# A recurrence and a gated mixture on one core: the mixture's U half decoded and begun first, V of three blocks later from operands kept in DRAM

## The chip, the cores and the metric

One core of a Trainium2 chip runs the whole program. Its engines are TensorE (PE, matrix products, with its weight loads shown apart as PEld), VectorE (DVE), ScalarE (ACT) and GpSimd (POOL); SyncE (SP) issues most of the DMA transfers. The metric is the device time of one execution in microseconds (us), lower is better. The times given are those of several runs of the same kernel; one further execution was recorded by the profiler.

## The reference

Two stages, one feeding the other. The first is a linear recurrence over 768 tokens, for 4 batches and 8 heads of 40 channels, with a 40x40 state:

```python
for t in range(S):
    y[:, :, t] = einsum('bhd,bhde->bhe', r_t, state)
    Sa = einsum('bhde,bhe->bhd', state, a_t)
    state = state * w_t[:, :, None, :] - einsum('bhd,bhe->bhde', Sa, b_t)
    state = state + einsum('bhd,bhe->bhde', v_t, k_t)
x = y.transpose(0, 2, 1, 3).reshape(4, 768, 320)
```

The second is a gated mixture on x. The hidden layer's first 512 columns are U, the other 512 are V:

```python
h = maximum(x @ w_in, 0)                 # (4, 768, 1024)
u, v = h[..., :512], h[..., 512:]
v_n = (v - mean(v)) / sqrt(var(v) + 1e-6)
v_s = einsum('ts,bsd->btd', w_spatial, v_n) + b_spatial[None, :, None]
return (u * v_s) @ w_out                 # (4, 768, 320)
```

The product with w_spatial mixes all 768 tokens of a batch, so it can begin for a batch only when V of the rows that it reads is there, and its result is multiplied by U.

## The kernel before, in words

*Phase 1.* The tokens are cut into chunks of 64. A step (0 to 23) handles one chunk for two batches at once: 12 steps for batches 0 and 1, 12 for batches 2 and 3. Eight heads stand as 4 pairs, so a step has 8 units (2 batches x 4 head pairs), the two heads of a pair on the two halves of the partitions.

Three kinds of work belong to a chunk. Its *preparation*: loads (prep_piece), running products on VectorE (scan1, scan2), at_mul and sl_mul, then a product of 32x32 blocks on TensorE (lprime) whose result lblock copies from a PSUM bank to the tile Lc on VectorE, multiplied by the table maskl, which is -1 below the diagonal and 0 elsewhere. For four chunks together invert(g) then inverts these triangles on VectorE, in 30 pairs of a multiply and an add with one transpose ahead and two behind: its result XT is read by b_zt. Then the *block work* b_... of the chunk, on TensorE with copies on ScalarE and triangles cut out by GpSimd. Last the *chain* c_..., which alone hangs on the step before: c_bp (the state enters), c_ff, c_xx, c_mp (the state leaves as Mc) and c_y, each followed by its copy. y, the recurrence's output, is stored to the DRAM tensor xs by y_store, every second step, for 128 tokens. c_ff reads the tiles Rt and At; a part of Rt is the token load vtok_load, which goes from DRAM straight into it.

*The mixture's first layer.* A block is 128 tokens of one pair of batches: 12 blocks, and block j can be loaded after step 2j+1. m_load brings x from xs with six loads (tile xt), m_split cuts it into a high and a low part (xh on ScalarE, xl and the rest of xh on GpSimd), and then come four U products (m_u, a slot of 8 matmuls into a bank) and two V products (m_v, 8 wider matmuls). Both go to the tile pv or itmp. U is stored to the DRAM tensor uts; V is normalised (m_n1, m_root, m_n2, m_n3) and stored to vns. The weights w_in come as pairs of words and are decoded into wh and wl by six generators of eight pieces each, V's three first, one in a step from 4.2 on; only after all six does open_act open the pool in which the blocks' tiles stand. There are 72 slots for these products, at the times of M1 to M4 of each step from 11 on, four a step: 52 of them fall in steps 11 to 23, and 20 at times of 24 and later.

*What sets the order.* Phase 1's order is written out by hand: at(t, fn) puts calls into the list plan, which is sorted by t (the number ahead of the point is the step), and runs through it, issuing to each engine in that order. Each engine, and SyncE's queue, works its own instructions in the order in which they were issued. Entries with t of 24 and more are issued outside the hand-written part, and there a scheduler of the framework interleaves them with phase 2 by its own estimate.

*Phase 2.* For each of four batches and two halves of 384 tokens: spatial (72 products of vh, vl with the split w_spatial into the banks pg, then bias and U on VectorE, split again) and proj (36 products with w_out, tile po), whose result ot is stored once for a half. vload brings V of a batch by six row blocks (raw), splits them on ScalarE (vh) and GpSimd (vl), and loads U (ut).

The lines that the prediction names: L179 to L181 the three products of spatial, L199 the products of proj and L201 the output's store, L339 lprime, L349 lblock, L363, L367 and L372 the inversion, L384 the token load, L406 the triangles on GpSimd, L468 b_l21, L487 b_zt, L545 c_bp, L563 c_ff, L581 c_xx, L654 c_y's copy, L666 y_store, L685 and L689 m_load, L712 m_v, L759 m_u, L776 the copy xf, L51 and L55 the two splits, wherever they are called from.

## Time and profile before

| what | value |
| --- | --- |
| time, median of 3 runs | 667.46 us (665.67 to 667.48) |
| the profiled execution's own time | 665.08 us |
| its span | 663.3 us, mean granted clock 0.943 |
| busy: TensorE, VectorE, ScalarE, GpSimd | 571.8, 448.4, 384.2, 225.9 us |
| first product of step 0, 1, 7, 11, 12, 23 | 32.2, 65.5, 186.8, 255.1, 278.4, 476.6 us |
| y of step 23 written | 490.0 us |
| first product of proj, last product | 546.4, 659.2 us |

The span is the time from the first to the last recorded instruction; the time of a run is a little longer. A step's beginning is read from the first product of c_bp. Busy time of PE counts products whose ends are modelled. The granted clock is TensorE's, as a share of full speed. In a row of the groups, what stands behind the second bar is the idle time of the engine just before these instructions, and what ended it.

### The profile page before, as it was taken

To read this page: it belongs to the slowest core of one execution; us is meant where nothing else is said; L and a number is where in the kernel's file an instruction comes from. 1 tells how busy PE (TensorE), PEld (TensorE's weight loads), DVE (VectorE), ACT (ScalarE), POOL (GpSimd) and SP (SyncE) were. 2 spreads that over 40 slices of the span, in tenths; PEclk is the share of its full clock that TensorE was granted. 3 is DMA by queue.
4 is the path that set the end of the run, shared out by engine and by line. 5 is a ranking of instruction groups with operands and counts; after the bars stand their busy time and mean duration, and the time that the engine had idled before them with its cause. 6 is when DMAs were issued, how large, how long until landed. Compare 5 with 4: busy or idle time off the path is not lost.

```text
span 663.3 us, 25848 instructions
## 1 busy us (share of the span) xinstructions
PE 571.8 (86%) x10960; PEld 518.3 (78%) x10960; DVE 448.4 (68%) x970; ACT 384.2 (58%) x860; POOL 225.9 (34%) x298
## 2 busy tenths in 40 slices
PE   1447885498777887999999999999989999999997
PEld 1437674487766776888888888888878999999997
DVE  8999789989999999488896677343384842332220
ACT  2135662377666775688878887888765543221212
POOL 6013330224332334144341332332354843352221
PEclk9967997789787898999999999999998999999999
DMA  8654778477555546657565365375395557150001
GB/s 199 121 107 67 134 152 147 70 175 155 135 127 115 131 117 120 142 127 172 154 190 148 86 173 144 90 198 132 89 262 182 162 155 240 61 157 31 31 31 59
DMA packets 106331, 87.68 MB, mean 132 GB/s; under 512 B 35496, under 2 KB 92072, under 8 KB 104296
## 3 DMA queue, kind: packets, MB, share of 16 engines
q1 hardware_dynamic: 105672, 84.31, 52.0%
q10 hardware_dynamic: 544, 1.72, 1.2%
q8 instruction: 86, 1.41, 1.0%
q14 instruction: 29, 0.24, 0.1%
HBM read 59.20 MB, written 20.50 MB: 120 GB/s over the span
## 4 chain that ended last, share of the span: by engine, by line
PE 63%; DVE 15%; DMA 7%; issue 6%; ACT 4%; SPq 3%; POOL 1%; DVEq 0%; ACTq 0%; POOLq 0%
PE po L199 6%; PE pv L759 6%; PE pv L712 6%; PE pg L179 5%; PE pg L180 5%; PE pg L181 5%; PE ch L563 4%; PE bp L545 4%; PE ch L581 4%; PE bk L429 2%; DMA ein<-in_early 2%; DVE itmp L363 2%; PE bk L451 2%; PE bk L399 2%; PE bp L641 2%
## 5 line engine op out<-in xcount | busy, mean ns | idle before, releaser
L406 POOL TENSOR_SCALAR_AFFINE_SELECT Rt<-Rt 64x512 f32<-64x512 f32 (+1 forms) x144 | 83.8, 584 | 156.2 <-ACT Rt L592 128.5
L406 POOL TENSOR_SCALAR_AFFINE_SELECT At<-At 64x512 f32<-64x512 f32 x48 | 41.5, 864 | 164.0 <-ACT At L416 151.9
L555 ACT ACTIVATE Rt<-bp 64x416 f32<-64x416 f32 x96 | 49.1, 511 | 56.2 <-PE bp L545 53.6
L363 DVE TENSOR_TENSOR itmp<-A 128x30 f32<-128x30 f32 (+9 forms) x180 | 66.5, 369 | 3.4
L179 PE MATMUL pg<-wsh,vh 128*128 128x384 f32 x192 | 65.4, 341 | 2.0 <-ACT vh L51 2.0
L545 PE MATMUL bp<-lin,Mc 40*64 40x104 f32 x768 | 47.3, 278 | 22.1 <-DVE y L654 19.8
L183 DVE TENSOR_TENSOR g<-pg,bb 128x384 f32<-128x384 f32 x32 | 17.8, 556 | 70.7 <-PE pg L181 68.4
L180 PE MATMUL pg<-wsl,vh 128*128 128x384 f32 x192 | 65.1, 339 | 0.0
L181 PE MATMUL pg<-wsh,vl 128*128 128x384 f32 x192 | 63.6, 339 | 0.0
L367 DVE TENSOR_TENSOR A<-A,itmp 128x30 f32<-128x30 f32 (+9 forms) x180 | 59.1, 328 | 6.2
L545 PEld LDWEIGHTS bp<-lin,Mc 40*64 40x64 f32 x768 | 40.7, 150 | 25.5 <-DVE y L654 22.7
L563 PE MATMUL ch<-Rt,At 128*64 128x104 f32 x768 | 48.0, 283 | 5.9 <-issue 4.8
L55 POOL TENSOR_TENSOR gl<-g,gh 128x384 fp32r<-128x384 f32 x32 | 33.0, 1035 | 58.1 <-ACT gh L51 58.1
L592 ACT ACTIVATE Rt<-ch 64x416 f32<-64x416 f32 x96 | 49.1, 511 | 4.6 <-PE ch L581 2.2
L563 PEld LDWEIGHTS ch<-Rt,At 128*64 128x64 f32 x768 | 42.2, 157 | 10.4 <-issue 7.1
L51 ACT ACTIVATE gh<-g 128x384 fp32r<-128x384 f32 x32 | 16.7, 521 | 54.3 <-DVE g L184 54.3
L339 PE MATMUL bk<-at,sl 64*32 64x32 f32 x1536 | 21.2, 203 | 26.5 <-DVE sl L324 20.7
L55 POOL TENSOR_TENSOR vl<-raw,vh 128x512 fp32r<-128x512 f32 x24 | 31.5, 1324 | 31.6 <-ACT vh L51 30.1
L581 PE MATMUL ch<-ffs,xf 64*64 64x104 f32 x768 | 41.7, 261 | 0.0
L339 PEld LDWEIGHTS bk<-at,sl 64*32 64x32 f32 x1536 | 17.7, 114 | 29.5 <-issue 14.4
L179 PEld LDWEIGHTS pg<-wsh,vh 128*128 128x128 f32 x192 | 36.6, 190 | 2.4 <-ACT vh L51 2.2
L630 DVE TENSOR_TENSOR Mc<-ch,scn 104x160 f32<-104x160 f32 x44 | 18.5, 436 | 29.0 <-PE ch L619 18.7
(132 smaller groups left out, 1497.8 us busy)
## 6 DMA issues: line engine op xcount, KB each, us to landing
ein<-in_early SPq DMA_DIRECT2D x108, 129.0 KB
lin<-in_late SPq DMA_DIRECT2D x48, 160.0 KB
At<-at SPq DMA_DIRECT2D x48, 128.0 KB
uts<-ur SPq DMA_DIRECT2D x48, 128.0 KB
vns<-vr SPq DMA_DIRECT2D x24, 256.0 KB
raw<-vns SPq DMA_DIRECT2D x24, 256.0 KB
ut<-uts SPq DMA_DIRECT2D x24, 256.0 KB
Rt<-in_vtok SPq DMA_DIRECT2D x48, 80.0 KB
```

The lines of the kernel that those rows point to most:

```text
L55: eng.tensor_tensor(out=lo, in0=x, in1=hi.bitcast(F32), op=ALU.subtract)
L179: nc.tensor.matmul(pg, lhsT=vh[:, dc], rhs=w_h, start=(i == 0), stop=False)
L180: nc.tensor.matmul(pg, lhsT=vh[:, dc], rhs=w_l, start=False, stop=False)
L181: nc.tensor.matmul(pg, lhsT=vl[:, dc], rhs=w_h, start=False, stop=(i == NT - 1))
L363: nc.vector.tensor_tensor(out=tp, in0=A[:, k + 1:, k:k + 1].broadcast_to([P, m, k]), in1=A[:, k:k + 1, 0:k].broadcast_to([P, m, k]), op=AL ...
L367: nc.vector.tensor_tensor(out=A[:, k + 1:, 0:k], in0=A[:, k + 1:, 0:k], in1=tp, op=ALU.add)
L406: nc.gpsimd.affine_select(out=t, in_=t, pattern=[[0, k], [1, C]], base=0, channel_multiplier=-1, compare_op=ALU.is_gt, fill=0.0,)
L545: nc.tensor.matmul(bp[PR[par], q, :], lhsT=Mc[RR[par], n, :], rhs=li[RR[par], n, C:], start=(q == 0), stop=False, skip_group_check=True,)
L555: nc.scalar.activation(Rt[par][PR[par], gp, :], st["bp", g][PR[par]], AF.Copy)
L563: nc.tensor.matmul(ff[PR[1 - par], q, :], lhsT=At[par][:, n, :], rhs=Rt[par][:, n, :], start=True, stop=True,)
L581: nc.tensor.matmul(xx[ev, q, :], lhsT=xf[ev, n, :], rhs=ffs[ev, q, :], start=True, stop=True,)
L592: done = nc.scalar.activation(Rt[par][PR[par], gp], xx[PR[1 - par]], AF.Copy, scale=-1.0)
```

## The change

Six things are changed; all else that the diff shows follows from them.

1. *Decoding and pools.* U's three weight decodes come first (at 3.83, 4.43 and 5.69), V's three later (7.02, 8.2 and 9.6), from a pool of their own. The blocks' pool opens after the first three, a second one for V's tiles after the other three.
2. *U of blocks 0 to 2 first.* Twelve slots are new, from 7.8 to 10.9, and hold all U products of blocks 0 to 2. V of these blocks comes behind the U and V of blocks 5, 6 and 8 (the list ORDER). For that m_keep stores xh and xl of such a block to the DRAM tensor xsp (640 KB), and m_again loads them again. From step 11 on there are four slots a step as before, so that 64 fall ahead of step 24 and 8 behind; the last six are put at 24.8 or later.
3. *Triangles.* lblock is a copy on ScalarE with the factor -1, without the table. The upper triangle is zeroed instead inside invert: five memsets on A after the first transpose, on VectorE for the first group, on GpSimd for the others.
4. *Idle products.* beat issues 10 products of ident with itself (512 columns, result unused) at 0.415, ahead of b_zt of chunk 0.
5. *Times of the preparation.* The tables PREP, LPQ, GAP, INV_T and OV set when the later chunks are prepared and inverted; scr_store of the first chunks moves ahead.
6. *Output stores.* Each 128 rows of the output are stored by themselves, 24 stores for 8.

Branches that were never taken (for example the VectorE variant of c_xx_out) are taken out of the text, which changes no instruction.

```diff
-        nc.sync.dma_start(
-            out=out[b, h * TH:(h + 1) * TH].rearrange("(j p) n -> p j n", p=P), in_=ot
-        )
+            t0 = h * TH + j * P
+            nc.sync.dma_start(out=out[b, t0:t0 + P], in_=ot[:, j, :])
...
+    J_U = 3
+    xsp = dscr.tile([J_U, P, 5, NB, P], F32, name="xsp")
...
-        nc.vector.tensor_tensor(
-            out=Lc[:, u0:u0 + NU, :], in0=st.pop(("pl", s)),
-            in1=maskl.unsqueeze(1).broadcast_to([P, NU, HB]), op=ALU.mult,
-        )
+        nc.scalar.activation(Lc[:, u0:u0 + NU, :], st.pop(("pl", s)), AF.Copy, scale=-1.0)
...
-        A = inv.tile([P, HB, HB], F32, name="A")
+        Af = inv.tile([P, HB * HB + HB], F32, name="A")
+        A = Af[:, 0:HB * HB].rearrange("p (t s) -> p t s", s=HB)
         nc.vector.transpose(out=A, in_=Lc.rearrange("p u t -> p t u"))
+        h = HB // 2
+        while h:
+            x = Af.rearrange("p (b x) -> p b x", x=2 * h * (HB + 1))[:, :, h:h + h * HB]
+            (nc.gpsimd if g else nc.vector).memset(x.rearrange("p b (r c) -> p b r c", c=HB)[:, :, :, 0:h], 0.0)
+            h //= 2
...
+    def m_keep(j, *key):
+        xh, xl = st["xhl", key]
+        nc.sync.dma_start(out=xsp[j, :, 0:3], in_=xh.bitcast(F32))
+        nc.sync.dma_start(out=xsp[j, :, 3:5], in_=xl.bitcast(F32))
+
+    def m_again(j, *key):
+        xh = st["act"].tile([P, 3, NB, P], F32R, name="xh", bufs=2)
+        xl = st["act"].tile([P, 2, NB, P], F32R, name="xl", bufs=2)
+        nc.sync.dma_start(out=xh.bitcast(F32), in_=xsp[j, :, 0:3])
+        nc.sync.dma_start(out=xl.bitcast(F32), in_=xsp[j, :, 3:5])
+        st["xhl", key] = (xh, xl)
...
-        vr = st["act"].tile([P, DH], F32, name="vr", bufs=2)
+        vr = st["actv"].tile([P, DH], F32, name="vr", bufs=3)
...
+    def beat(k):
+        for _ in range(k):
+            nc.tensor.matmul(
+                st["beat"], lhsT=ident, rhs=ident.unsqueeze(1).broadcast_to([P, 4, P]), start=True, stop=True
+            )
...
+    for t, k in [[0.415, 10]]:
+        at(t, beat, k)
...
-    T_DEC, T_MOE = 4.2, 11
-    for i in range(6):
-        gen = decode(1 - i // 3, i % 3)
-        for k in range(8):
-            at(T_DEC + i + k * 0.10 - (0.9 if k == 0 else 0), step, gen)
-    at(T_DEC + 5.9, open_act)
-    slots = [T_MOE + k // 4 + (M1, M2, M3, M4)[k % 4] for k in range(3 * NS)]
+    T_DEC, T_DECV, T_MOE = (3.83, 4.43, 5.69), (7.02, 8.2, 9.6), 11
+    for half, t_dec, dk, lead in ((0, T_DEC, 0.08, 0.9), (1, T_DECV, 0.08, 0.45)):
...
+    slots = [7.8, 8.3, 8.55, 8.8, 9.3, 9.46, 9.8, 9.85, 10.3, 10.55, 10.7, 10.9]
+    slots += [T_MOE + k // 4 + (M1, M2, M3, M4)[k % 4] for k in range(3 * NS - len(slots))]
+    slots[-6:] = [max(t, NS + 0.8 + 0.05 * k) for k, t in enumerate(slots[-6:])]
...
-    for j in range(NS // 2):
+    ORDER = [("u", j) for j in range(J_U)]
+    for j in range(J_U, NS // 2):
+        ORDER += [("uv", j)] + [("v", k) for k, a in enumerate((5, 6, 8)) if a == j]
...
-        own = slots[6 * j:6 * j + 6]
-        at(max(own[0] - 1.6, 2 * j + 2.1, T_DEC + 5.92), m_load, bq, i)
-        at(max(own[0] - 0.45, 2 * j + 2.7), m_split, bq, i)
+        if kind == "v":
+            at(own[0] - 0.8, m_again, j, bq, i)
+        else:
+            at(max(own[0] - 0.9, 2 * j + 2.1, T_DEC[2] + 7 * 0.08 + 0.02, slots[4 * J_U - 4] - 0.4 if j == J_U else 0), m_load, bq, i)
+            at(max(own[0] - 0.5, 2 * j + 2.7), m_split, bq, i)
...
+        if kind == "u":
+            at(own[0] + 0.3, m_keep, j, bq, i)
...
```

How the order moves, at three places. The first is TensorE in step 9, between c_ff and c_xx of the chain (before: L563 is c_ff, L451 and L468 are block work of chunk 10, L581 is c_xx, L487 is b_zt of chunk 10). Before:

```order
L563 MATMUL ch<-Rt_134,At_3447 64x104
L563 MATMUL ch<-Rt_135,At_3448 64x104
L451 MATMUL bk<-ident,sl 128x128 x8
L468 MATMUL bk<-sl,at 32x32 x16
L581 MATMUL ch<-ffs,xf_131 64x104 x16
L487 MATMUL bk<-XT_3281,l_3919 32x32 x16
```

And now (L552 is c_ff, L440 and L457 are the block work, L570 is c_xx, L757 is a U slot):

```order
L552 MATMUL ch<-Rt_131,At_3499 64x104
L552 MATMUL ch<-Rt_132,At_3500 64x104
L440 MATMUL bk<-ident,sl 128x128 x8
L757 MATMUL pv<-xh,wh 128x256 x3
L757 MATMUL pv<-xl,wh 128x256 x2
L757 MATMUL pv<-xh,wl 128x256 x3
L457 MATMUL bk<-sl,at 32x32 x16
L570 MATMUL ch<-ffs,xf_128 64x104 x16
```

A U slot of eight products now stands among the block work, ahead of c_xx.

The second is SyncE's queue behind the y of step 23 (L666 stores y, L685 and L689 load a block, L154 loads a row block of V for phase 2, L762 stores U, L749 stores V, L164 loads U for phase 2). Before:

```order
L666 DMA xs<-y_8628 40x4x128 x2
L666 DMA xs<-y_8638 40x4x128 x2
L154 DMA raw<-vns 128x512 x2
L762 DMA uts<-ur 128x256
L164 DMA ut_9398<-uts 128x4x128
L749 DMA vns<-vr 128x512
L685 DMA xt<-xs 128x2x128
L749 DMA vns<-vr 128x512
L689 DMA xt<-xs 64x128
L762 DMA uts<-ur 128x256 x2
L689 DMA xt<-xs 64x128
```

And now (L645 stores y, L671 and L675 load a block, L760 stores U, L747 stores V):

```order
L645 DMA xs<-y_8901 40x4x128 x2
L645 DMA xs<-y_8911 40x4x128 x2
L671 DMA xt<-xs 128x2x128
L675 DMA xt<-xs 64x128 x2
L671 DMA xt<-xs 128x2x128
L675 DMA xt<-xs 64x128 x2
L760 DMA uts<-ur 128x256
L747 DMA vns<-vr 128x512 x2
L154 DMA raw<-vns 128x512 x2
```

The last block's six loads now stand straight behind the stores of y on which they wait, and the loads of V's row blocks behind them.

The third is TensorE after step 23, inside spatial of the first batch, ahead of the first product on row block 2 of V (vh02). Before, where xh_8815 is the third last block, block 9:

```order
L181 MATMUL pg1_9479<-wsh0_9268,vl00_9365 128x384
L179 MATMUL pg1_9479<-wsh1_9274,vh01_9370 128x384
L180 MATMUL pg1_9479<-wsl1_9275,vh01_9370 128x384
L181 MATMUL pg1_9479<-wsh1_9274,vl01_9371 128x384
L759 MATMUL pv_8858<-xh_8815,wh_138 128x256 x3
L759 MATMUL pv_8858<-xl_8816,wh_138 128x256 x2
L759 MATMUL pv_8858<-xh_8815,wl_139 128x256 x3
L179 MATMUL pg0_9407<-wsh2_9280,vh02_9376 128x384
```

And now, where xh_9119 is the last block, block 11:

```order
L181 MATMUL pg1_9533<-wsh1_9328,vl01_9425 128x384
L757 MATMUL pv_9124<-xh_9119,wh_135 128x256 x2
L757 MATMUL itmp_9136<-xh_9119,wh_135 128x256 x2
L757 MATMUL pv_9124<-xh_9119,wh_135 128x256
L757 MATMUL pv_9124<-xl_9120,wh_135 128x256 x2
L757 MATMUL pv_9124<-xh_9119,wl_136 128x256 x3
L757 MATMUL itmp_9136<-xh_9119,wh_135 128x256
L757 MATMUL itmp_9136<-xl_9120,wh_135 128x256 x2
L757 MATMUL itmp_9136<-xh_9119,wl_136 128x256 x3
L179 MATMUL pg0_9461<-wsh2_9334,vh02_9430 128x384
```

U products of the last block now stand ahead of the first product on vh02, where there stood one of block 9.

More of the change, by code (lines that the diff above doesn't have):

```diff
@@ L847, in phase1 @@
             at(t0 + (t1 - t0) * k / (INV_N - 1), step, gen)
-    T_DEC, T_MOE = 4.2, 11
-    for i in range(6):
-        gen = decode(1 - i // 3, i % 3)
-        for k in range(8):
-            at(T_DEC + i + k * 0.10 - (0.9 if k == 0 else 0), step, gen)
-    at(T_DEC + 5.9, open_act)
-    slots = [T_MOE + k // 4 + (M1, M2, M3, M4)[k % 4] for k in range(3 * NS)]
+    T_DEC, T_DECV, T_MOE = (3.83, 4.43, 5.69), (7.02, 8.2, 9.6), 11
+    for half, t_dec, dk, lead in ((0, T_DEC, 0.08, 0.9), (1, T_DECV, 0.08, 0.45)):
+        for i in range(3):
+            gen = decode(half, i)
+            for k in range(8):
+                at(t_dec[i] + k * dk - (lead if k == 0 else 0), step, gen)
@@ new lines, in phase1 @@
+    for j in range(J_U, NS // 2):
+        ORDER += [("uv", j)] + [("v", k) for k, a in enumerate((5, 6, 8)) if a == j]
+    n = 0
+    for kind, j in ORDER:
+        bq, i = j // 6, j % 6
+        own = slots[n:n + {"u": 4, "v": 2, "uv": 6}[kind]]
+        n += len(own)
+        if kind == "v":
[3 more added lines that the diff above has]
+            at(max(own[0] - 0.5, 2 * j + 2.7), m_split, bq, i)
+        us = {"u": own, "v": [], "uv": [own[k] for k in (0, 1, 3, 4) if k < len(own)]}[kind]
+        vs = {"u": [], "v": own, "uv": own[2::3]}[kind]
+        for t, d in zip(us, range(DH // P)):
@@ L883, in pads @@
         eng.memset(t[:, WF:], 0.0)
+    st["beat"] = ps_m.tile([P, DH], F32, name="pv")
     with tc.manual_schedule():
@@ L890, in phase1 @@
         pads(v, ein[1])
-        p.memset(maskl, -1.0)
-        for q in range(P // HB):
-            rows = slice(q * HB, (q + 1) * HB)
-            p.affine_select(
-                out=maskl[rows], in_=maskl[rows], pattern=[[1, HB]], base=0,
-                channel_multiplier=-1, compare_op=ALU.is_gt, fill=0.0,
-            )
         pads(p, ein[2])
@@ L937, in phase1 @@
         prep_load(4, 48)
-        for q in range(GS):
-            scr_store(q)
         b_lka(0)
```

131 lines of the change are left out of this document (54 added, 77 removed).

## The prediction

> **What bounds the kernel now.** I read first the busy times by stretch, cut at the first product of a step (step 0 begins at 32.2, step 1 at 65.5, step 11 at 255.1, step 23 at 476.6), then the waits, then the chain of waits, then the instructions in order of time around three places. The stretches (columns: stretch, length, busy time and count of TensorE products, weight loads, VectorE, ScalarE, GpSimd, granted clock, DMA share, GB/s):
>
> ```profile
> 32.20:65.50 33.30, 20.29 (x477) 18.36 (x474) 30.62 (x64) 15.61 (x37) 9.40 (x10) 0.64 0.50 88
> 65.50:186.80 121.30, 89.48 (x2664) 78.60 (x2656) 108.17 (x210) 71.75 (x164) 36.00 (x49) 0.89 0.70 137
> 186.80:255.10 68.30, 57.02 (x1600) 50.43 (x1600) 66.25 (x132) 48.75 (x111) 21.56 (x33) 0.90 0.50 120
> 278.40:476.60 198.20, 197.26 (x4350) 170.91 (x4344) 129.34 (x335) 161.58 (x365) 67.77 (x104) 1.00 0.53 142
> 489.30:541.80 52.50, 50.55 (x299) 48.34 (x298) 34.75 (x84) 27.78 (x60) 30.15 (x26) 0.97 0.59 176
> 541.80:663.30 121.50, 117.42 (x721) 117.03 (x719) 30.20 (x56) 29.31 (x61) 37.70 (x35) 1.00 0.29 94
> ```
>
> Up to step 10 VectorE sets the pace: 66.25 of 68.30 us busy in steps 7 to 10, while TensorE has 11.3 us idle there. From step 12 on TensorE is busy 197.26 of 198.20 us, and it stays the bound to the end: every product that leaves it after 278 is time. The waits of VectorE from 58 to 256 and of TensorE from 58 to 283, and the group that the first belong to:
>
> ```profile
> DVE Lc L349 <- PE bk L339: 4.0, 4, 1.8
> DVE Mc L630 <- ACT Rt L592: 2.3, 2, 1.4
> PE bk L468 <- DVE Lc L349: 5.2, 1, 5.2
> L349 DVE TENSOR_TENSOR Lc<-bk,maskl 128x256 f32<-128x256 f32 x24 | 10.1, 419 | 5.5 <-PE bk L339 5.5
> ```
>
> The copy Lc stands in VectorE's way twice: it costs 0.419 us, and VectorE waits in front of it for its product; once TensorE in turn waited 5.2 us for the bank that Lc empties.
>
> **The change, part by part.** The sum is made against the profiled execution's 665.1 us (span 663.3).
>
> *Triangles to ScalarE.* Fifteen of the 24 copies lie between 65 and 255 (1 in step 11, 4 before step 0, 4 after): 15 x 0.419 = 6.3 us leave VectorE, and with them up to 4.0 us of waits. On ScalarE a copy costs about 0.41 (next row), 0.4 us a step beside 12 to 13 busy of 18, so other work hides it; without that cover it would be the same 6 us. The zeroing runs on GpSimd (busy 21.56 of 68.30) and is needed only by the transpose at the inversion's end; group 0's, on VectorE, is 496 columns, at 485 ns for 512 about 0.6 us, and replaces four Lc of the prologue: even. I take -6.3: bounds -10.3 (the waits go too) and 0, since in steps 1 to 6 VectorE is idle for 13 of 121 us and so not always the one that is late.
>
> The copies xf of the same size on ScalarE, the one timed zeroing of 512 columns, and four more stretches (steps 8 to 11):
>
> ```profile
> L776 ACT ACTIVATE xf<-XT 128x256 f32<-128x256 f32 x24 | 9.9, 413 | 11.6 <-DVE XT L372 11.4
> L881 DVE MEMSET ein<- 128x512 f32 x1 | 0.5, 485 | 0.0
> 205.30:223.30 18.00, 16.00 (x432) 14.31 (x432) 17.51 (x36) 12.98 (x30) 5.53 (x8) 0.81 0.70 157
> 223.30:241.50 18.20, 14.63 (x402) 12.91 (x402) 17.65 (x36) 12.59 (x28) 4.83 (x8) 0.91 0.39 86
> 241.50:255.10 13.60, 12.79 (x400) 11.32 (x400) 13.05 (x29) 11.48 (x27) 5.46 (x9) 1.00 0.44 120
> 255.10:278.40 23.30, 18.48 (x362) 16.22 (x362) 14.21 (x26) 12.53 (x29) 6.90 (x10) 0.85 0.75 141
> ```
>
> *Twelve U products early.* One falls in step 7, three in step 8, four each in 9 and 10. A U takes 0.95 to 1.14 us, a V 1.85 to 2.04 (chain, below). TensorE's idle time: 2.0 us in step 8 (needs 2.9), 3.6 in step 9 (needs 3.8), 0.8 in step 10 (needs 3.8). Excess 4.1; the half-clock stretches of these steps (0.81, 0.91) will shrink as TensorE fills, so I take +3.5. Bounds 0 and +5.
>
> From the chain of waits (start, length, engine, tile and line; L712 are V's products, L759 are U's):
>
> ```profile
> 257.08 6.47 DMA Rt<-in_vtok
> 263.68 3.00 PE ch L563 x30
> 271.29 2.04 PE pv L712 x8
> 274.42 1.14 PE pv L759 x8
> 493.81 4.06 DMA raw<-vns
> 503.89 1.85 PE pv L712 x8
> 505.74 0.95 PE itmp L759 x8
> 518.14 0.17 PE pg L179
> ```
>
> *Step 11.* It lasts 23.3 us. The instructions in order of time show c_ff (L563) standing 4.5 us (3.42 and 1.12) for the second token load of step 11, issued only at 257.08, behind the six loads of the first block; step 10's had been issued at 234.77, 6.7 us ahead of that step:
>
> ```profile
> 261.99 0.58 PE L563 MATMUL ch<-Rt,At 128*64 128x104 f32 x2 [3.42 <-issue]
> 263.68 0.62 PE L563 MATMUL ch<-Rt,At 128*64 128x104 f32 x4 [1.12 <-DMA Rt<-in_vtok]
> 234.77 0.59 SPq L384 DMA_DIRECT2D Rt<-in_vtok  x1
> ```
>
> Now the first block loads come four steps earlier, and step 10 is 3 us longer, so the token load has more time. I take -4.0; bounds -5.7 (a step of 17.6) and +4.5 (the new stores and reloads, 640 KB a block, hold it up as much again).
>
> *Steps 12 to 23.* 52 slots before held 35 U and 17 V, now 31 and 21: 4 x 0.9 = +3.6.
>
> *After step 23.* 13 U and 6 V stood there, now 5 and 2: 8 x 0.95 + 4 x 1.85 = -15.0 us of TensorE's own work. But the cover of a chain goes with it. The last block's U wait for y of step 23, its store, the block load and the split. Rows:
>
> ```profile
> 489.24 0.75 DVE L654 TENSOR_TENSOR y<-bp,Et 104x256 f32<-104x256 f32 x2
> 491.48 2.23 SPq L666 DMA_DIRECT2D xs<-y  x4
> 476.23 0.39 SPq L685 DMA_DIRECT2D xt<-xs  x1
> 478.49 1.12 SPq L689 DMA_DIRECT2D xt<-xs  x2
> 481.22 0.85 ACT L51 ACTIVATE xh<-xt 128x768 fp32r<-128x768 f32 x1 [0.38 <-DMA xt<-xs]
> 483.55 0.87 POOL L55 TENSOR_TENSOR xh<-xt,xh 64x256 fp32r<-64x256 f32 x1
> 497.04 0.39 SPq L685 DMA_DIRECT2D xt<-xs  x1
> 511.32 0.83 ACT L51 ACTIVATE xh<-xt 128x768 fp32r<-128x768 f32 x1
> 498.57 0.44 PE L179 MATMUL pg<-wsh,vh 128*128 128x384 f32 x1 [1.95 <-ACT vh L51]
> ```
>
> On the old times: y ends at 490.0; four stores take 2.2 to issue (492.2) and about 2 to land (from the last xt issue's end at 479.61 to xh 1.6; a raw load in the chain 4.06): 494.2. A block's first load to its last operand (476.23 to 484.42) is 8.2: ready at 502.4. TensorE comes to the last block's first U after 24 gating products of 0.17 (chain, 518.14) and one U, at 489.4 + 4.1 + 0.95 = 494.5, and stands until 502.4: 7.9 us. Behind it in TensorE's order stand all further gating products; in ScalarE's, vh of row blocks 2 to 5 stands behind this xh; on SyncE their loads stand behind the block load. The old wait of 1.95 at this place is covered by it, so +5.9, and +1 for a longer time at half clock: +6.9. Bounds +2 (only xh must wait, 4.0 net of the old wait) and +14 (a load like the last one of before, 497.04 to 511.32).
>
> *Idle products.* Before step 0's first product on X, TensorE stands while VectorE inverts, and then runs at half clock:
>
> ```profile
> 52.45 1.06 PE L487 MATMUL bk<-XT,l 32*32 32x32 f32 x32 [12.27 <-DVE XT L372]
> 56.42 3.04 PE L581 MATMUL ch<-ffs,xf 64*64 64x104 f32 x32
> 75.24 1.64 PE L581 MATMUL ch<-ffs,xf 64*64 64x104 f32 x32
> ```
>
> Sixteen products of 104 columns take 1.6 at full and 3.0 at half clock, two running at once, so one of 512 columns by estimate 1.0 or 1.9, ten 10 or 19: against 12.3 idle they fit only if the clock rises under them. The gain is 1.4 + 0.5 at most, and VectorE is busy 30.62 of 33.30 there: I take -0.7, bounds -1.9 and +7. [...]
>
> *Output stores per 128 rows.* The end waits for the last store; a third of its size saves, by estimate, 0.5 of the 3.6 us from its issue at 659.7 to 663.3.
>
> ```profile
> 659.72 0.37 SPq L201 DMA_DIRECT2D out_y<-ot  x1
> ```
>
> *The rest.* The decodes are the same instructions in another order, the preparation of later chunks moves by up to a third of a step, and the mask tables leave GpSimd's prologue. I cost them at nothing: VectorE's other work hides the prologue's, and the counts stay; bounds -1 and +1, VectorE's idle time in steps 8 and 9 together (0.49 and 0.55).
>
> Sum: -6.3 + 3.5 - 4.0 + 3.6 - 15.0 + 6.9 - 0.7 - 0.5 = -12.5, so 652.6 in a run like the profiled one. That one lies 2.4 below the median of the runs shown (667.5) and 0.6 below the lowest; I take half of it: **653.5**.
>
> **Rivals.** (1) *The wait after step 23 eats the tail.* For it: SyncE issues the load straight behind the stores, and DMA is 59% busy there. Against it: a load at 476 took 5.0 to xh in the same crowd. With +14 for +6.9: 661. (2) *More at the front.* VectorE's waits go with the copies, the U products fit, the new wait is at its lower bound: 653.5 - 4.0 - 3.5 - 4.9 = 641.1. For it: the 5.2 us wait for Lc goes with it; against: step 10 has no idle time on TensorE. (3) *Nothing at the front*: the chain through ScalarE and GpSimd bounds steps 0 to 11, not VectorE. Then 653.5 + 6.3 + 4.0 + 0.7 = 664.5. Against: 97% busy in steps 7 to 10. (4) *Slower: the token load comes late in every step that keeps or reloads a block.* One mechanism, step 11's: 640 KB stand in SyncE's queue and in the rings ahead of the load c_ff needs. Six steps, 4.5 us each, and step 11's gain lost: 653.5 + 27 + 4 = 684. It turns the sum from three such steps on (12.5 / 4.5). Against: step 10's load went out 6.7 us ahead of its step, and the order of the queue keeps that lead except where block traffic stands in front.
>
> **How the numbers follow.** Forecast 0.54, own range 647 to 659 (the front's bounds and the tail's, half of each); (1) 0.14, (2) 0.14, (3) 0.08, (4) 0.10. Two times of this kernel nearer than 0.3% can't be told apart. Faster: the forecast, (1), (2) and half of (3), 0.86; same 0.04; slower 0.10. Range 642 to 665: it leaves out (4) and half of (2), 0.17.
>
> **What would show it.** VectorE without Lc, and steps 5 to 9 some 0.4 us shorter each; step 10 near 16.5 and step 11 near 18; steps 12 to 22 0.3 longer; a wait of 5 to 10 us for xh on TensorE some 5 us after step 23's last product, a stretch at half clock behind it; 8 fewer U and 4 fewer V from there to the first projection. Wrong if c_ff waits for token loads in several steps, if the ten idle products end after X, or if the wait is missing.

## The result and the profile after

The changed kernel is slower: 677.59 us (median of 14 runs, 669.47 to 681.87) against 666.73 us (14 runs, 660.87 to 669.38). The ratio is 1.0124, with a 95% interval of 1.0093 to 1.0155; it leaves out the five executions of the changed kernel that lie over 1.5% above its fastest, while the medians take in all (677.59 / 666.73 is 1.0163). The forecast was 653.5 us in a range of 642 to 665, so its sign was wrong.

The profiled execution took 669.47 us (span 667.7), the fastest of the 14; its stages therefore explain 4.4 us of a loss of 8 to 11. The changed kernel was profiled once more in the experiments (span 669.2). Stage lengths of the three profiles, cut at the first product of c_bp as in the prediction:

(The -6.3 us of the triangles are spread over steps 1 to 10 in the last column.)

| stage | before | after | after, again | forecast of the change |
| --- | --- | --- | --- | --- |
| up to step 1 | 65.5 | 67.3 | 65.7 | -0.7 |
| steps 1 to 6 | 121.3 | 123.3 | 126.0 | about -4 |
| steps 7 to 10 | 68.3 | 77.0 | 77.1 | about +1 |
| step 11 | 23.2 | 20.0 | 19.3 | -4.0 |
| steps 12 to 22 | 198.2 | 204.3 | 204.6 | +3.6 |
| step 23 to the end | 186.7 | 175.9 | 176.5 | -8.6 |

The last three rows went about as forecast. The loss is at the front: step 12 begins at 287.5 and 288.1 where it began at 278.4. The stretches of the changed kernel (stretch, length, busy time and count of TensorE, weight loads, VectorE, ScalarE, GpSimd, clock, DMA share, GB/s):

```profile
29.63:67.27 37.64, 29.54 (x498) 21.85 (x494) 33.06 (x70) 15.36 (x37) 7.92 (x10) 0.74 0.54 91
67.27:190.55 123.28, 94.33 (x2600) 82.16 (x2593) 107.00 (x204) 76.14 (x174) 33.81 (x58) 0.84 0.66 132
190.55:267.58 77.03, 69.22 (x1696) 60.19 (x1696) 66.58 (x125) 57.62 (x129) 28.98 (x43) 0.96 0.70 164
267.58:287.53 19.95, 17.19 (x426) 15.08 (x425) 13.90 (x24) 12.09 (x27) 6.11 (x11) 1.00 0.83 182
287.53:491.80 204.27, 201.53 (x4346) 172.52 (x4344) 133.86 (x362) 167.92 (x379) 66.88 (x112) 1.00 0.54 149
511.70:522.00 10.30, 6.62 (x25) 6.32 (x26) 0.19 (x1) 2.87 (x5) 4.52 (x4) 0.50 0.52 164
```

VectorE's idle time in steps 1 to 10 rose: it is busy 107.00 + 66.58 of 200.3 us, where the same steps before took 189.6 us with 174.5 busy. What was taken off VectorE did not shorten the steps. Nor did TensorE stand longer there: it was idle for 43.1 us of them before (189.6 less 146.5 busy) and for 36.8 after. What grew is its busy time, by 17.1 us. 12.2 of these lie in steps 7 to 10, where the U products stand. The other 4.9 lie in steps 1 to 6, where it had 64 products fewer to do: its granted clock was 0.84 there instead of 0.89. The second profile of the changed kernel has the same (94.9 us busy at 0.85).

TensorE's longest waits in steps 1 to 4, before and after (engine, tile and line that waited, what ended it, total, times, longest):

```profile
PE bp L545 <- DVE y L654: 8.3, 2, 4.5
PE bk L468 <- DVE Lc L349: 5.2, 1, 5.2
PE bk L339 <- issue: 4.6, 4, 1.9
PE bk L451 <- ACT tk L457: 2.9, 1, 2.9
PE ch L563 <- issue: 0.6, 1, 0.6
```

```profile
PE bp L534 <- DVE y L633: 7.1, 3, 5.1
PE bp L620 <- issue: 5.4, 2, 3.0
PE bk L440 <- ACT tk L446: 4.7, 2, 4.5
PE bk L337 <- issue: 1.6, 1, 1.6
PE bk L400 <- issue: 1.3, 1, 1.3
PE ch L598 <- issue: 1.1, 1, 1.1
PE bk L457 <- issue: 0.9, 1, 0.9
```

"issue" is time in which the engine waited for nothing that the profile shows. Before, 5.2 us of it, nearly all inside lprime (L339), which no later link of the chain needs at once. After, 10.3 us, and 5.4 of them inside c_y (L620), a link of the chain. One such place in step 4, in order of time: the last of c_y's products stands alone for 2.96 us, and VectorE's y waits for it.

```profile
149.96 1.09 PE L620 MATMUL bp<-Rt,tk 128*40 128x64 f32 x31
154.01 0.33 PE L620 MATMUL bp<-Rt,tk 128*40 128x64 f32 x1 [2.96 <-issue]
154.38 0.42 DVE L633 TENSOR_TENSOR y<-bp,Et 104x256 f32<-104x256 f32 x1 [2.42 <-PE bp L620]
```

What TensorE waits for there is seen by counting its recorded instructions (products, weight loads and a few semaphore instructions) in order, and by looking at the DMA queue that the page calls "instruction". From the page of the changed kernel (queue, packets, MB, share):

```profile
q8 instruction: 86, 1.41, 1.0%
```

1.41 MB in 86 packets are 16 KB each. TensorE has 22,090 recorded instructions before and 22,134 after, and 22,090 / 256 is 86.3: one packet for 256 instructions. Counted from the records, for some of the stalls (end of the stall, line, its length, number of TensorE's instructions ahead of it, remainder by 256, end of the queue's last packet):

```
before  73.25 L339 lprime 1.87  1985 193   71.58
before 100.02 L339 lprime 1.25  3521 193   98.24
before 150.67 L339 lprime 0.95  5313 193  148.97
after   73.04 L337 lprime 1.64  1985 193   71.40
after   86.55 L400 b_lka  1.29  2753 193   85.09
after  102.74 L620 c_y    2.40  3521 193  101.23
after  154.01 L620 c_y    2.96  5313 193  152.48
after  170.00 L620 c_y    1.04  6081 193  168.00
```

So these are stalls for code. In the 20 profiles of this case there are 146 "issue" stalls of TensorE of 0.6 us or more between 60 and 300 us; 145 of them stand at an instruction whose number leaves 193 by 256, 1.2 to 3.1 us (median 1.5) behind the end of a packet of that queue. At the 673 block ends without such a stall the packet had ended earlier, 3.2 us ahead in the median. The one that doesn't (10,393, remainder 153) is c_ff of step 11 in the kernel before, for the token load, as the prediction had read it. The block ends 3521 and 5313 fell into lprime before and fall into c_y now. With the ten idle products (40 recorded instructions) taken out again, the second falls back into lprime and the first stays in c_y; both the idle products and the new order of the rest move them. Between 60 and 300 us the stalls for code come to 7.8 us before, and to 11.3 and 17.1 in the two profiles of the changed kernel. They are one part of TensorE's idle time, which was not longer on the whole; how much of the loss is theirs is not shown.

### The profile page after: what moved, and what is told of

The parts are those of the page before. It is cut to its first block, busy times and chain, and to the rows that moved or that the text cites. A ratio compares the mean times of both kernels' runs of the same rounds, so it can differ in the third digit from the quotient of the medians.

```text
span 667.7 us, 25915 instructions
## 1 busy us (share of the span) xinstructions
PE 587.4 (88%) x10980; PEld 522.9 (78%) x10980; DVE 438.6 (66%) x951; ACT 395.3 (59%) x884; POOL 220.4 (33%) x312
## 3 DMA queue, kind: packets, MB, share of 16 engines
q8 instruction: 86, 1.41, 1.0%
## 4 chain that ended last, share of the span: by engine, by line
PE 63%; DVE 15%; ACT 9%; DMA 5%; issue 4%; SPq 3%; POOL 0%; ACTq 0%; DVEq 0%; POOLq 0%
PE po L199 6%; PE pv L710 6%; PE pv L757 5%; PE pg L180 5%; PE pg L179 5%; PE pg L181 5%; PE ch L570 4%; PE bp L534 4%; PE ch L552 4%; DVE itmp L364 3%; DVE A L368 3%; PE bk L424 2%; PE bp L620 2%; DMA ein<-in_early 2%; PE ch L598 2%
## 5 line engine op out<-in xcount | busy, mean ns | idle before, releaser
L407 POOL TENSOR_SCALAR_AFFINE_SELECT Rt<-Rt 64x512 f32<-64x512 f32 (+1 forms) x144 | 80.8, 561 | 176.1 <-ACT Rt L580 143.7
L407 POOL TENSOR_SCALAR_AFFINE_SELECT At<-At 64x512 f32<-64x512 f32 x48 | 39.4, 820 | 131.0 <-ACT At L416 128.8
L364 DVE TENSOR_TENSOR itmp<-A 128x30 f32<-128x30 f32 (+9 forms) x180 | 71.1, 395 | 3.4
L552 PE MATMUL ch<-Rt,At 128*64 128x104 f32 x768 | 44.4, 264 | 5.7 <-DMA Rt<-in_vtok 3.7
L552 PEld LDWEIGHTS ch<-Rt,At 128*64 128x64 f32 x768 | 37.8, 142 | 10.6 <-issue 5.4
L570 PE MATMUL ch<-ffs,xf 64*64 64x104 f32 x768 | 42.2, 261 | 0.0
L337 PE MATMUL bk<-at,sl 64*32 64x32 f32 x1536 | 22.0, 212 | 21.2 <-DVE sl L322 19.3
L570 PEld LDWEIGHTS ch<-ffs,xf 64*64 64x64 f32 x768 | 36.8, 139 | 1.4
```

Of the source, the lines that this page charges most:

```text
L364: nc.vector.tensor_tensor(out=tp, in0=A[:, k + 1:, k:k + 1].broadcast_to([P, m, k]), in1=A[:, k:k + 1, 0:k].broadcast_to([P, m, k]), op=AL ...
L407: nc.gpsimd.affine_select(out=t, in_=t, pattern=[[0, k], [1, C]], base=0, channel_multiplier=-1, compare_op=ALU.is_gt, fill=0.0,)
L552: nc.tensor.matmul(ff[PR[1 - par], q, :], lhsT=At[par][:, n, :], rhs=Rt[par][:, n, :], start=True, stop=True,)
L570: nc.tensor.matmul(xx[ev, q, :], lhsT=xf[ev, n, :], rhs=ffs[ev, q, :], start=True, stop=True,)
```

## The experiments

Ratios are to the kernel before, on the same chip, from up to 28 executions of it and 6 to 12 of the other, with 95% intervals. Four chips were used, and the changed kernel itself was timed again beside the first four runs alone; the intervals reach 0.3 to 0.6% to each side, so a smaller difference between two ratios is not told apart. A profile is one execution.

**The changed kernel again.** No edit.

> The changed kernel as it is, so that the others can be set against it on the same chip. Theory A (the early U products with their loads and stores hold up the chain in steps 8 to 11, more in some executions than in the profiled one): 1.008 to 1.016 of before, and a profile of a longer execution shows the surplus in steps 8 to 13. Theory B (the idle products and the clock behind them): the surplus is in steps 0 and 1, where the stretch at half clock is longer still. Theory C (triangles on ScalarE): it is spread over steps 0 to 18.

1.0150 [1.0115, 1.0185], 676.3 us. Steps 7 to 10 took 77.1 us again, steps 1 to 6 took 126.0, the time up to step 1 65.7. The surplus of the longer executions could not be placed: this profiled one, too, was the shortest of its six.

**Idle products.** Five kernels. Taken out of the changed kernel:

```diff
-    for t, k in [[0.415, 10]]:
-        at(t, beat, k)
```

> The changed kernel without the ten idle products. Theory B: step 0 shrinks from 37.6 to about 33.5, the whole by 4 us or 0.6%, to about 1.006 of before. Theories A and C: step 0 changes by less than 1.5 us, since VectorE's inversion and not TensorE ends the wait there, and the ratio stays at 1.010 to 1.013.

1.0101 [1.0060, 1.0143]: 0.5% less, though the intervals overlap. The length of step 0 does not decide it: 34.1 us here, but 37.6 and 34.0 in the two profiles with the idle products. As many instructions without their time:

```diff
+    def tiny(k):
+        for _ in range(k):
+            nc.tensor.matmul(st["beat"][:, 0:2], lhsT=ident, rhs=ident[:, 0:2], start=True, stop=True)
...
-        at(t, beat, k)
+        at(t, tiny, k)
```

> The changed kernel with ten products of 2 columns in place of the ten of 512 columns: as many instructions on TensorE, no time. In the profiles so far TensorE's stalls that nothing explains end at every 256th of its instructions (place 193 of 256), 1.5 us behind a transfer of 16 KB in the instruction queue. Theory K (the 40 instructions move these places into c_y): as the changed kernel, 1.012 to 1.016. Theory T (the idle products' time or the clock behind them): as without them, 1.008 to 1.011.

1.0147 [1.0096, 1.0199], as the changed kernel, though the interval takes in most of that of the run without idle products. The stalls stand in c_y again (3.32 us at instruction 3521, 3.78 at 5313). The idle products with 54 small ones behind them, together a whole block of 256 instructions:

```diff
         at(t, beat, k)
+        at(t + 0.001, tiny, 54)
```

> The changed kernel with its ten idle products and 54 products of 2 columns behind them, 256 instructions in all, so that every later instruction stands at the place in its block of 256 that it has without idle products. Theory K: as without idle products, 1.008 to 1.011, and stalls at c_ff and lprime in place of c_y. Theory T: 1.012 to 1.016.

1.0358 [1.0316, 1.0400]. Neither theory had this, and the run doesn't test them: the small products were not free. Each recorded product took 185 ns, 20 us in all, near the 190 ns of one weight load of ident in the profile of the changed kernel, so that b_zt began at 63.6 instead of 51.8:

```profile
43.69 19.98 PE L773 MATMUL pv<-ident 128*128 128x2 f32 x108
63.60 1.07 PE L476 MATMUL bk<-XT,l 32*32 32x32 f32 x32
```

Then the same two edits on the kernel before, which has nothing else of the change:

```diff
+    at(0.415, tiny, 10)
```

> The kernel before with ten products of 2 columns at 0.415 and nothing else. Theory K: the stalls at lprime in steps 2 and 4 move into c_y; 2 to 5 us slower, 1.003 to 1.008. Theory T: no change, 0.998 to 1.002.

```diff
+    at(0.415, beat, 10)
```

> The kernel before with the ten idle products of 512 columns at 0.415 and nothing else. Theory K: as with the ten small ones, 1.003 to 1.008. Theory T: the only one of the two that is slower, 1.004 to 1.008. Prediction as made: 0.997 to 1.000 (0.7 us gained).

The small ones: 1.0032 [1.0005, 1.0059]; the idle ones: 1.0095 [1.0063, 1.0127]. So the prediction's gain of 0.7 us is a loss of some 6 us when the idle products come alone. Ten products that compute nothing, and take 2.3 us out of the 12.3 that TensorE was idle there, cost 0.3%, the lower end of what theory K gave. Of the two stalls that it moves into c_y, one is there in the profile (1.28 us at instruction 5313) and one stayed in lprime (2.74 us at 3521). The stalls for code come to 16.8 us there, 9 more than before, yet this profiled execution took 664.53 us, no longer than the one of the kernel before (665.08): their sum is not a price. The rest of the 0.95%, and why only about half of it shows inside the changed kernel, is not explained. In the profile of the run with idle products step 1 begins at 64.65, 0.9 us earlier than before, as the prediction said. Against the small ones' profile its loss stands in steps 5 to 11, where lprime stood 4.12 us for code at 228.3. Against the kernel before, TensorE's products of steps 1 to 10 were busy 150.8 us instead of 146.5, at a granted clock of 0.87 instead of 0.89.

**U of blocks 0 to 2 first.** Undone:

```diff
...
-    J_U = 3
+    J_U = 0
...
-    slots = [7.8, 8.3, 8.55, 8.8, 9.3, 9.46, 9.8, 9.85, 10.3, 10.55, 10.7, 10.9]
+    slots = []
...
```

> The changed kernel with all U and V products from step 11 on, block by block as before (no early slots, no copy of operands kept); decodes in the new order, triangles on ScalarE and idle products stay. Theory A: step 11 begins 7 to 10 us earlier (near 258 instead of 267.6) and steps 12 to 22 lose 4, while the end after step 23 gets some 11 longer, so the profiled total is within 3 us of the changed kernel's best run, and the runs no longer scatter by 12 us: about 1.003 of before. Theories B and C: the front keeps its loss and the 11 us at the end come on top: 1.02 or more.

1.0106 [1.0066, 1.0146]. By stages it is what theory A said: steps 7 to 10 take 66.0 us instead of 77.0, step 12 begins at 278.4, the end after step 23 is 188.2 us instead of 176, steps 12 to 22 take 199.9. The scatter stayed (667.65 to 676.89), so that part of the theory fell, and so did its ratio of 1.003. The early products alone, on weights, without what hangs on them (on top of the edits of the run before):

```diff
...
+    def idle_u():
+        pv = ps_m.tile([P, DH], F32, name="pv")
+        for i in range(8):
+            nc.tensor.matmul(
+                pv[:, 0:NB * P], lhsT=wh[:, i % 3, 0:P], rhs=wl[:, i % 3, 0:NB * P], start=(i == 0), stop=(i == 7)
+            )
+
+    for t in [7.8, 8.3, 8.55, 8.8, 9.3, 9.46, 9.8, 9.85, 10.3, 10.55, 10.7, 10.9]:
+        at(t, idle_u)
...
```

> The changed kernel without early U as in the run before (1.0106), plus twelve idle groups of eight products of 256 columns on weights alone at the twelve early times, with no block load, no split, no copy and no store. Theory A2a (TensorE's time in the chain is the price): 5 to 8 us more than without them, 1.019 to 1.022. Theory A2b (it is what hangs on the products: loads, ScalarE's splits and copies, stores): at most 2 us more, 1.010 to 1.014.

1.0200 [1.0143, 1.0256], 0.9% above the run without them (1.0106 [1.0066, 1.0146]). Steps 7 to 10 of four profiles: without early U, with the products alone, with all of it but the kept operands (next run), and the changed kernel's second profile:

```profile
192.46:258.45 65.99, 56.22 (x1600) 49.16 (x1600) 63.30 (x124) 51.40 (x115) 23.31 (x37) 0.93 0.75 137
```

```profile
195.38:267.11 71.73, 68.25 (x1697) 59.71 (x1697) 64.50 (x126) 51.59 (x115) 26.10 (x39) 0.95 0.62 127
```

```profile
191.62:268.26 76.64, 68.70 (x1696) 59.70 (x1696) 65.42 (x127) 57.32 (x129) 28.35 (x44) 0.97 0.68 150
```

```profile
191.74:268.88 77.14, 70.98 (x1697) 62.05 (x1697) 65.95 (x127) 57.66 (x129) 28.15 (x43) 0.93 0.71 164
```

The products add 12.0 us of TensorE time and make the four steps 5.7 us longer: half of them finds idle time. What hangs on them (loads, ScalarE's splits and copies, stores) adds 5 us more, by these profiles. VectorE's busy share falls from 0.96 to 0.85 along these rows, so it is not what stretches the steps. Without the stores and reloads of the kept operands:

```diff
...
+        st["last"] = key
...
     def m_keep(j, *key):
         xh, xl = st["xhl", key]
-        nc.sync.dma_start(out=xsp[j, :, 0:3], in_=xh.bitcast(F32))
-        nc.sync.dma_start(out=xsp[j, :, 3:5], in_=xl.bitcast(F32))
...
     def m_again(j, *key):
...
-        nc.sync.dma_start(out=xh.bitcast(F32), in_=xsp[j, :, 0:3])
-        nc.sync.dma_start(out=xl.bitcast(F32), in_=xsp[j, :, 3:5])
-        st["xhl", key] = (xh, xl)
+        st["xhl", key] = st["xhl", st["last"]]
```

> The changed kernel without the stores and reloads of the kept operands: V of blocks 0 to 2 is computed from the operands of the block that stands in the tiles at that time (so the output's V is another one). Theory A1 (the traffic of 640 KB a block, twice, stands ahead of the loads that the chain and ScalarE wait for): steps 8 to 11 and 15, 17, 20 get shorter, 5 to 8 us in all, to about 1.005 of before. Theory A2 (the early products themselves, with their block loads, splits and copies): less than 2 us, 1.012 to 1.015.

1.0104 [1.0050, 1.0158], between the two theories, and steps 7 to 10 are no shorter (76.6). The kept operands are not what holds up these steps, and whether they cost anything elsewhere is within the noise; the chain of waits of the changed kernel shows there the block loads' neighbours, the token loads and the stores of U for which ScalarE's next copy of U waits:

```profile
230.37 2.73 DMA Rt<-in_vtok
248.47 4.17 DMA Rt<-in_vtok
266.43 4.34 DMA uts<-ur
```

**Both undone.** The edits of the first kernel and of the one without early U.

> The changed kernel without early U and without the idle products. If the two losses add, 4 us less than either alone: 668, about 1.004 of before. If the idle products' loss was scatter (the two intervals overlap), it stays at 1.009 to 1.011.

1.0065 [1.0029, 1.0102]: 0.4% less than either alone, as if the two losses add, though the intervals overlap; 0.65% were left.

**Triangles.** Back on VectorE in the changed kernel (with maskl, without the five memsets):

```diff
-        nc.scalar.activation(Lc[:, u0:u0 + NU, :], st.pop(("pl", s)), AF.Copy, scale=-1.0)
+        nc.vector.tensor_tensor(
+            out=Lc[:, u0:u0 + NU, :], in0=st.pop(("pl", s)),
+            in1=maskl.unsqueeze(1).broadcast_to([P, NU, HB]), op=ALU.mult,
+        )
```

> The changed kernel with the triangles copied by VectorE with the mask, as before, without the zeroing on GpSimd. Theory C: ScalarE no longer has the copy ahead of the chain's copies and steps 1 to 11 get 3 to 6 us shorter: about 1.005 of before. Theories A and B: VectorE gets 0.42 us a step back, steps 1 to 7 get up to 3 us longer or nothing changes: 1.012 to 1.017.

1.0162 [1.0121, 1.0204]: no difference that can be told. And the other way round, the triangles on ScalarE in the kernel before:

```diff
-        nc.vector.tensor_tensor(
-            out=Lc[:, u0:u0 + NU, :], in0=st.pop(("pl", s)),
-            in1=maskl.unsqueeze(1).broadcast_to([P, NU, HB]), op=ALU.mult,
-        )
+        nc.scalar.activation(Lc[:, u0:u0 + NU, :], st.pop(("pl", s)), AF.Copy, scale=-1.0)
...
+            scr_store(q)
             at_mul(q, v)
...
```

> The kernel before with the triangles on ScalarE, the zeroing in the inversion, and scr_store of the first chunks moved ahead (without which ScalarE's order blocks). Prediction as made: 6.3 us less, 0.991. Theory that VectorE's freed time only becomes idle time, because the chain goes through ScalarE, TensorE's order and the code blocks: 0.998 to 1.003.

1.0045 [1.0009, 1.0081]: slower, where 0.991 was predicted, and a little above what the other theory gave. Steps 1 to 10 before, and with the triangles on ScalarE, and ScalarE's copy there:

```profile
65.51:255.14 189.63, 146.48 (x4265) 129.04 (x4257) 174.47 (x341) 120.54 (x275) 57.59 (x82) 0.89 0.63 131
```

```profile
65.45:260.22 194.77, 151.63 (x4265) 133.88 (x4257) 169.57 (x327) 126.69 (x290) 58.52 (x97) 0.87 0.63 128
L349 ACT ACTIVATE Lc<-bk 128x256 f32<-128x256 f32 x15 | 5.8, 384 | 11.6 <-PE bk L339 11.4
```

VectorE's busy time fell by 4.9 us, close to the 6.3 of the prediction, and its idle time rose by 10. The wait for lprime's product moved with the copy: ScalarE, which carries three of the chain's copies (behind c_bp, c_ff and c_xx), now stands 11.4 us ahead of Lc. That this costs the chain is not shown. TensorE, by the same rows, was idle for 43.1 us in both. The lengthening of 5.1 us is all in its busy time, for the same products, at a granted clock of 0.87 instead of 0.89. Its two longest waits for VectorE there, before and then:

```profile
PE bp L545 <- DVE y L654: 19.8, 11, 4.5
PE bk L468 <- DVE Lc L349: 5.2, 1, 5.2
```

```profile
PE bp L548 <- DVE y L657: 17.9, 11, 4.2
PE bk L490 <- DVE XT L375: 5.9, 1, 5.9
```

The wait for Lc is gone, a wait of about its size for the inversion's result XT is there instead, and the wait for y is nearly what it was.

**Preparation times and decodes.** The tables as before, all else as changed:

```diff
...
+    PREP = {4: 0.03, 5: 0.45, 6: 1.03, 7: 1.45, 8: 2.03, 9: 2.45, 10: 3.03, 11: 3.45}
+    LPQ, INV_T = {}, {1: (2.5, 3.7), 2: (4.5, 7.7)}
+    GAP = {4: 0.03, 5: 0.03, 6: 0.03, 7: 0.03}
+    OV = {(scr_store, 4): 0.68, (sl_mul, 5): 0.83}
```

> The changed kernel with the times of preparation and inversion as before (the tables PREP, LPQ, GAP, INV_T, OV undone). Theory P (the new times put VectorE's and ScalarE's work where the chain of steps 3 to 7 waits for it): 3 us less, about 1.010. Otherwise the tables fit the rest of the change and undoing them costs: 1.015 to 1.020.

1.0129 [1.0074, 1.0184]: can't be told from the changed kernel. Then four parts undone at once (early U, idle products, triangles, tables):

> The changed kernel without early U, without idle products, with the triangles on VectorE and the preparation times as before: of the change only the decode order with its pools, the earlier scr_store of the first chunks, the output stores and the later block loads are left. If triangles and times cost the rest: 0.997 to 1.003 of before. If the decode order or the pools do: 1.005 to 1.008 as without early U and idle products alone.

1.0098 [1.0064, 1.0131]: not less than with two parts undone (1.0065; the intervals overlap). With two parts undone and V decoded first, at the old spacing:

```diff
-    T_DEC, T_DECV, T_MOE = (3.83, 4.43, 5.69), (7.02, 8.2, 9.6), 11
-    for half, t_dec, dk, lead in ((0, T_DEC, 0.08, 0.9), (1, T_DECV, 0.08, 0.45)):
+    T_DEC, T_DECV, T_MOE = (4.2, 5.2, 6.2), (7.25, 8.2, 9.2), 11
+    for half, t_dec, dk, lead in ((1, T_DEC, 0.08, 0.9), (0, T_DECV, 0.08, 0.45)):
...
```

> The changed kernel without early U and without idle products, with V decoded first at 4.2, 5.2 and 6.2 and U at 7.25, 8.2 and 9.2. If two decodes within step 4 (VectorE is busy 18.4 us there instead of 14.0) cost the rest: 1.000 to 1.003 of before. Otherwise 1.005 to 1.008.

1.0192 [1.0135, 1.0249], against both expectations. And with four parts undone and only the spacing of the decodes as before:

```diff
-    T_DEC, T_DECV, T_MOE = (3.83, 4.43, 5.69), (7.02, 8.2, 9.6), 11
+    T_DEC, T_DECV, T_MOE = (4.2, 5.2, 6.2), (7.25, 8.2, 9.2), 11
```

> The changed kernel with early U, idle products, triangles and preparation times undone (the run that was 1.0098 of before), and with the decodes one a step again: U at 4.2, 5.2 and 6.2, V at 7.25, 8.2 and 9.2. If two decodes in step 4 (24.6 us long there, 17.3 before) cost the rest: 1.001 to 1.005 of before and step 4 under 20 us. If it is the order itself, the pools, the earlier scr_store or the later block loads: 1.008 to 1.012.

1.0112 [1.0071, 1.0154]. Step 4 is 18.2 us instead of 24.6, but the whole is no faster: two decodes in one step were not the cause. What is left in this kernel (the decode order with its pools, the earlier scr_store, block loads 0.9 of a step ahead instead of 1.6, last slots at 24.8, the output stores) costs 1% and was not taken apart.

**The token load of step 11, and a faster kernel.** On the kernel before, the two token loads of step 11 go ahead of the first block's loads:

```diff
-            at(q - 1 + 0.48 + 0.14 * par, vtok_load, q, par)
+            at(10.05 + 0.02 * par if q == 11 else q - 1 + 0.48 + 0.14 * par, vtok_load, q, par)
```

> The kernel before with the two token loads of step 11 issued at 10.05, ahead of the first block's loads, and nothing else. If c_ff of step 11 waited for them: step 11 is 18 to 19 us long and the whole 4 us less, 0.993 to 0.996. If it waited for code or the wait only moves to the block's split: 0.998 to 1.002.

0.9986 [0.9952, 1.0020], not to be told from no change, though the profile, of the fastest of the twelve executions, shows the mechanism: step 11 took 15.9 us, TensorE busy throughout, where it had been 23.2 with c_ff standing 4.5.

```profile
257.25:273.13 15.88, 15.88 (x369) 14.17 (x361) 14.36 (x25) 11.94 (x28) 6.39 (x10) 1.00 0.68 148
```

With the output stores by 128 rows, the sixth part of the change, beside it:

> The kernel before with the token loads of step 11 ahead of the first block's loads and the output stored by 128 rows. If both gain what the profile shows (2 to 5 us at step 11, 0.5 us at the end): 0.992 to 0.997. If the stall at step 11 stands in the profiled execution alone: 0.998 to 1.001.

0.9941 [0.9915, 0.9968], 660.8 us against 665.8: faster than both kernels. Step 11 is short again (15.8 us).

How the 0.6% divides between the two edits is not settled; the intervals of the two runs overlap slightly.

## Why the prediction was wrong, point by point

*"Up to step 10 VectorE sets the pace."* This is the step that failed, and the terms at the front fell with it. 66.25 of 68.30 us busy was read as the bound, so that what leaves VectorE would leave the time. But VectorE works its queue in order (in the profile of the kernel before it stood 1.80 us for lprime's product ahead of the Lc of 73.54, and a scan, L292, for which no wait of its own is shown, began behind it at 73.88), and the inversion and preparation of later chunks fill it; the share says that there was work, not that the chain waited for all of it. With the triangles alone moved, VectorE had 4.9 us less to do and became idle for 10 us more, and TensorE stood as long as before (43.1 us). TensorE does wait for VectorE there, 19.8 us of the 43.1 for y, but with less work on VectorE they hardly shrank (17.9). What bounds steps 1 to 10 instead is only known in part: in-order waits for single results, the stalls for code, and how much of the stretch TensorE is granted half its clock.

*Triangles, -6.3.* Measured alone +0.45%, about +3 us (with the earlier scr_store that it needs), and no change when undone in the whole. "0.4 us a step beside 12 to 13 busy of 18, so other work hides it" counted ScalarE's time and not its order: the copy now stands 11.4 us for lprime's product with the chain's copies behind it. Whether that cost time is open: TensorE's idle time did not grow.

*Twelve U products early, +3.5.* Steps 7 to 10 are 8.7 us longer than before, and 11 longer than in the same kernel without early U. TensorE's busy time there grew by 12.2 us, near the twelve products' own time, but its idle time shrank by 3.5 only, where the sum counted on 8. The working by idle time was near for the products alone (excess 4.1 by the sum, 5.7 in the run with nothing but them). That half-clock stretches shrink as TensorE fills, for which 0.6 of the 4.1 was taken off, is not shown: the granted clock of steps 7 to 10 was 0.90 before, 0.96 and 0.93 in the changed kernel, and 0.93 without early U too. Missing was what hangs on them: 5 us for three blocks' loads, splits, copies and stores in ScalarE's and SyncE's order, costed at nothing.

*Idle products, -0.7.* Alone +0.95%. The working compared their time with the idle time; they fitted (8.75 of 16.7 us, at full clock throughout: 1.00 from 35.13 to 43.88), but 40 more instructions shift every later block of code, a mechanism that the prediction did not have, and the clock did not stay up until X was there. That the clock rises under them, without which the ten would not have fitted, stood there as the author's estimate. In the changed kernel, in order of time, the idle products (each recorded as two) and the first product behind them; and the stretches behind, with the clock:

```profile
35.13 8.75 PE L773 MATMUL pv<-ident 128*128 128x512 f32 x20
51.80 1.06 PE L476 MATMUL bk<-XT,l 32*32 32x32 f32 x32 [7.93 <-DVE XT L373]
```

```profile
53.00:56.00 3.00, 3.00 (x98) 2.81 (x96) 2.93 (x4) 2.20 (x7) 0.00 (x0) 0.50 0.00 0
...
65.00:68.00 3.00, 3.00 (x98) 2.78 (x96) 2.01 (x3) 1.08 (x3) 1.31 (x2) 0.50 0.65 151
68.00:71.00 3.00, 3.00 (x112) 2.80 (x109) 2.96 (x4) 2.33 (x5) 0.00 (x0) 1.00 0.95 134
```

They ended 7.9 us before X was there, and step 0 ran at half clock to its end. That end is this execution's: in the second profile of the same kernel they ended 5.8 us before X, and the clock was back at 59.3. In the kernel before with the idle products alone they ended 3.0 us before X, and step 1 began 0.9 us earlier: there the forecast gain is in the profile, and the loss comes later.

*Step 11, -4.0.* Near in the profiles: 20.0 and 19.3 us, 3.2 and 3.9 less. That the earlier block loads did it is not shown. In the second profile c_ff still waits 1.1 us for a token load, and step 11 takes 17.2 to 20.1 us in the kernels without early U, which load the first block in step 10, and 18.3 in the kernel before with ten small products: the 23.2 of the one profile before is the longest of all 20. That the median gains as much is not shown: the run that mends this load alone gave 0.14% with an interval across zero.

*Steps 12 to 22, +3.6.* +6.1 and +6.4. TensorE's busy time rose by 4.3, near the term; the other 1.8 are idle time that was not there before.

*After step 23, -15.0 + 6.9 - 0.5 = -8.6.* -10.8 and -10.2: the mechanism and nearly the size. The wait stands where it was put, and behind it the stretch at half clock of the row 511.70:522.00, 10.3 us long (before, the one stretch at 0.50 after step 23 was 3.4 us, 499.66 to 503.07). The 1 us in the 6.9 for a longer time at half clock was the author's estimate; no run shows what that time cost. Beside it 1.9 us less wait than said (5.1 and 0.9 for 7.9), and, as counted, 8 U and 4 V fewer from step 23's beginning.

```profile
514.46 0.80 PE L757 MATMUL pv<-xh,wh 128*128 128x256 f32 x2 [5.14 <-ACT xh L51]
...
516.61 0.58 PE L757 MATMUL pv<-xh,wh 128*128 128x256 f32 x1 [0.93 <-POOL xh L55]
```

*The rest, 0.* Not nothing: with the four large parts undone, 1.0% and 1.1% were left.

*Slips of the working*, too small to matter: 14 copies of Lc, not 15, lie between 65 and 255 (5.9 us); half of 2.4 on 652.6 gives 653.8.

Of the rivals, (3), given 0.08, was right that less work for VectorE gives nothing at the front. That the chain through ScalarE and GpSimd does is not shown: of TensorE's 43.1 us of idle time before, some 5.5 end with ScalarE and none with GpSimd. Its 664.5 was too low as well. Rival (4), the only one with the right sign, had a real mechanism of about a seventh of its size: TensorE waited for token loads in steps 7 to 10 of the profiled execution 3.7 us in all, not 4.5 in each of six steps.

```profile
PE ch L552 <- DMA Rt<-in_vtok: 3.7, 3, 1.9
```

What stays open: where the longer executions of the changed kernel lose their further 5 to 10 us, why the idle products cost less inside the changed kernel than alone, which of the small parts left in the last kernels costs the 1%, and what decides how long TensorE has half its clock in steps 1 to 10 (0.85 to 0.89 in the mean, for products that are busy 146.5 to 153.8 us with no early U among them). The parts do not add up: with triangles and tables undone the remainder did not become smaller.

## What to carry to other kernels

Before you take work off an engine because it is busy, look at what the chain waits for: in an in-order queue filled with work for later, freed time can become idle time, and an instruction moved to another engine brings its wait along. Read a stretch that became longer in three parts, the bound engine's own work, its idle time and its clock, before naming a cause. Work moved forward out of a stage where TensorE is the bound costs, at its new place, its products where they find no gap, and everything that is loaded, copied and stored for them. In a program of many small products, count where code blocks end: an edit that only shifts instructions can cost something (0.3% here), so small edits are timed alone, in many executions.
